# A fused retention and two-layer kernel: another order of products, sums and gates in the second layer, seven places for its weights, and fewer positions for preparing it

## The chip, the cores and the metric

One core of a Trainium2 chip runs the whole program. The metric is the device time of one execution in microseconds (us). TensorE is called PE below, VectorE DVE, ScalarE ACT, GpSimd POOL; SP is the engine whose queue issues nearly all transfers.

## What is computed

The reference, cut to what matters:

```python
# q, k, v: 4 batches, 8 heads, 576 tokens, 64 per head; x: 2304 tokens x 512
scores = q @ k.T / sqrt(64)
x = (scores * decay) @ v           # decay: causal, gamma(head) ** distance
h = x @ w_in;   x = relu(h) ** 2 @ w_out                  # 512 -> 2048 -> 512
h = x @ w_in2;  out = h * clip(h + 3, 0, 6) / 6 @ w_out2   # 512 -> 2048 -> 512
```

## The kernel before

**Precision.** A product keeps about float32 precision by splitting each operand into a high part (ACT copies it, rounded) and a low part (DVE or POOL subtracts, lines 200 and 201), and by adding three passes: high by high, high by low, low by high (`PASSES`). A "split" below is one such pair of instructions.

**Layer one** walks 64 positions i: four blocks of tokens (`FIRST`) by 16 chunks of 128 hidden channels. At position i, PE computes the hidden product `hps` of i (line 448) and then the output product `yps` of i - 2 (line 506). ACT makes relu, square and high part of i, DVE the low part `g` (line 477), then the split of the input weights `win` of i + 2. In the last three positions of a block the operands of the next block (`xring`, `xown`) are split too.

**Preparation.** Beside layer one, at the positions in `READY`, the weights of layer two are decoded from 64-bit numbers (`dec`: four DVE instructions, lines 179 to 194, and two on ACT), summed (`sums` on POOL, `out_sums` on DVE, lines 577 to 580), split into one of three places `ready`, and stored to DRAM (`kept`, `rights`). A pair of chunks takes four decodings, two groups of sums and eight splits. Each step has a cost in a planner's units (26 a decoding, 9 an output split, 176 a pair); the eight pairs' costs divided by the number of positions are the pace at which steps are handed out, in a fixed order.

**Layer two** uses a product scheme with seven products P1 to P7 in place of eight, in both of its matrix products, over three blocks j of 768 tokens. `hidden(j)` makes, for each of eight pairs p, seven products (line 723), combines them into `plain` and `mixed`, and closes them with the gate: `bend` (ACT, line 732) into a tile `v` of the pool `wo`, `close` (DVE, line 736). `sum_up(p)` (four DVE instructions, lines 674 and 677) then makes the summed operands. `plain` holds the operands of P1 and P2, which need no sums; P5 reads what the sums leave in `mixed`, and P6, P7 and P3 read `sums`. `visible(j)` runs the second seven products (line 870) in the order of `ORDER`, each in six entries s of 12 matmuls (left operand `gop`, split two entries ahead by `split_operand`) and four weight tiles of 512 KB (`load_right`, line 803), each used for one and a half entries. The pool `wo` has four places, which these weights share with `v`. Into the entries of `visible`, the lists `between` and `side` put other work: the last pair's gates and sums, and the operands and left weights (`load_left`, `win`, line 670) of the next block.

All instructions stand on their engines in the order in which the code writes them; an engine whose next instruction waits lets nothing behind it pass.

Of the kernel before, what the change touches and what calls it, by code (L numbers as in the profile page):

```python
# [9 lines left out]
F32 = mybir.dt.float32  # L10
# [12 lines left out]
HALF = 384  # L23
# [20 lines left out]

WARM = 18

READY = list(range(17, 59))

TOKENS = (("w4", "w5"), ("w6", "w7"), ("x4", "x5"), ("x6", "t7"), ("t0", "t1"), None, None)

# [27 lines left out]
def retention_moe_moe2(ctx, tc, qk, qk_last, kv, w_in, w_out, w_in2, w_out2, consts, out):  # L78
# [625 lines left out]


    def hidden(j, before):

        plain, mixed, sums = (later[x].tile([128, n, NPAIR, HALF], F32, tag=x, name=x) for x, n in
                              (("plain", 2), ("mixed", 2), ("sums", 3)))
        later["of", j] = {"P1": plain[:, 0], "P2": plain[:, 1], "P4": mixed[:, 0], "P5": mixed[:, 1],  # L710
                          "P6": sums[:, 0], "P7": sums[:, 1], "P3": sums[:, 2]}
        small = lambda k, p: dead(j, k)[:, HALF * (p % 2):HALF * (p % 2) + HALF]
        ta, tb, tc_, bent = {}, {}, {}, {}

        def product(p, name, to, first, last):
            k, half = LEFT[name]
            w = lefts[j, p, k] if k == 1 else lefts[j, p, k][:, half]
            x = operands[j, name]
            m = 0
            for f in range(2):  # L720
                o = slice(f * 128, f * 128 + 128)
                for wp, xp in PASSES:
                    nc.tensor.matmul(  # L723
                        out=to, lhsT=w[:, wp, o], rhs=x[:, xp, f],
                        start=first and m == 0, stop=last and m == 5, skip_group_check=True,
                    )
                    m += 1

        def bend(p, k):
            src = (plain, mixed)[k]  # L730
            v = bent[p, k] = wop.tile([128, 2, HALF], F32, tag="wo", name="v")
            nc.scalar.activation(out=v, in_=src[:, :, p], func=ACTF.Relu, bias=half_one, scale=1.0 / 6.0)  # L732

        def close(p, k):
            to = (plain, mixed)[k][:, :, p]
            nc.vector.scalar_tensor_tensor(
                out=to, in0=bent.pop((p, k)), scalar=1.0, in1=to, op0=ALU.min, op1=ALU.mult
            )

        def sum_up(p):  # L740
            less(sums[:, 1, p], plain[:, 0, p], mixed[:, 1, p])
            add(mixed[:, 1, p], mixed[:, 1, p], mixed[:, 0, p])
            less(sums[:, 0, p], mixed[:, 1, p], plain[:, 0, p])
            less(sums[:, 2, p], plain[:, 1, p], sums[:, 0, p])

        def fourth(p):
            product(p, "P4", ta[p], False, True)
            load_left(NPAIR * j + p + 2, 1) if p + 2 < NPAIR else None
            nc.scalar.activation(out=plain[:, 1, p], in_=ta[p], func=ACTF.Copy)
            bend(p, 0)  # L750

        def ahead(p, e):
            if p + 2 < NPAIR:
                load_left(NPAIR * j + p + 2, e)

        for p in range(NPAIR):
            ta[p], tb[p], tc_[p] = (bank(b + p % 2, [128, HALF], "hps") for b in (4, 2, 6))
            p1, p5, u2 = small(0, p), small(1, p), small(2, p)
            if p:
                bend(p - 1, 1)  # L760
            product(p, "P1", ta[p], True, False)
            nc.scalar.activation(out=p1, in_=ta[p], func=ACTF.Copy)  # L762
            if p > 1:
                sum_up(p - 2)
            product(p, "P5", tc_[p], True, False)
            nc.scalar.activation(out=p5, in_=tc_[p], func=ACTF.Copy)
            if p:
                close(p - 1, 1)
                fourth(p - 1)
            else:  # L770
                while unfinished:
                    unfinished.pop(0)()
            product(p, "P6", ta[p], False, False)
            nc.scalar.activation(out=u2, in_=ta[p], func=ACTF.Copy)
            if p:
                close(p - 1, 0)
            product(p, "P2", tb[p], True, True)
            ahead(p, 0)
            add(plain[:, 0, p], tb[p], p1)
            product(p, "P3", tc_[p], False, True)  # L780
            ahead(p, 3)
            add(mixed[:, 1, p], tc_[p], u2)
            product(p, "P7", ta[p], False, False)
            ahead(p, 2)
            add(mixed[:, 0, p], ta[p], p5)
            if p == NPAIR - 1:
                before()
        p = NPAIR - 1
        return [
            lambda: (bend(p, 1), sum_up(p - 1), close(p, 1)),  # L790
            lambda: (fourth(p), close(p, 0), sum_up(p)),
        ]

    ORDER = ["P1", "P5", "P6", "P2", "P7", "P3", "P4"]
    NQ = NPAIR // 2
    ENTRIES = NPAIR * HALF // 512
    FINAL = len(SECOND) - 1
    left_g, right_w = {}, {}

    def load_right(j, s):  # L800
        if s < len(ORDER) * NQ:
            w = wop.tile([128, 2, DM], F32R, tag="wo", name="wo")
            nc.sync.dma_start(out=w.bitcast(F32), in_=rights[s % NQ][:, ROW[ORDER[s // NQ]]])
            right_w[j, s] = w

    def split_operand(j, s):

        n, i = divmod(s, ENTRIES)
        if n >= len(ORDER):
            return  # L810
        if n < 4:
            t = place(f"w{i % 3}", [128, 2, 512], F32R, "gop")
        else:
            if (n, i) == (4, 0):
                later["entries"] = later["plain"].tile([128, ENTRIES, 2, 512], F32R, tag="plain", name="gop")
            t = later["entries"][:, i]
        left_g[j, s] = t
        src = later["of", j][ORDER[n]].rearrange("p a n -> p (a n)")[:, 512 * i:512 * i + 512]
        split_to(t[:, 0], t[:, 1], src, nc.vector)

    def visible(j, side, between):
# [38 lines left out]
        def multiply(n, u):  # L860
# [8 lines left out]
            for e, (gp, wp) in enumerate(PASSES):  # L869
# [3 lines left out]
                    stop=p == NPAIR - 1 and e == 2, skip_group_check=True,  # L873
                )

        due = {}
        for n, name in enumerate(ORDER):
            final = j == FINAL and n == len(ORDER) - 1
            for i in range(ENTRIES):
                s = n * ENTRIES + i  # L880
                if s + 2 < len(ORDER) * ENTRIES and s:
                    split_operand(j, s + 2)
                for f in due.pop(s, ()):
                    f()
                if final:
                    if i == 2:
                        for k in range(3, ENTRIES):
                            split_operand(j, n * ENTRIES + k) if (j, n * ENTRIES + k) not in left_g else None
                    continue
                for u in range(4 * i, 4 * i + 4):  # L890
                    multiply(n, u)
                    if u % 6 == 5:
                        load_right(j, n * NQ + u // 6 + 4)
                if s == 0:
                    split_operand(j, 2)
                if s < 2:
                    between[s]()
                for f in side.get(s, ()):
                    f()
            if not final:  # L900
                s = (n + 1) * ENTRIES
                due.setdefault(s, []).append(AFTER[name])
                if name in STORED:
                    due.setdefault(s + 3, []).extend(
                        lambda name=name, m=m: store(name, m, nc.sync) for m in range(3)
                    )
        if j == FINAL:
            n, name = len(ORDER) - 1, ORDER[-1]
            for m in range(3):
                for p in range(NPAIR):  # L910
                    multiply(n, 3 * p + m)
                one, two = spaces["a"]
                to = held(3)[:, m]
                if m == 1:
                    nc.vector.tensor_copy(to, one[:, 1])
                else:
                    nc.scalar.activation(out=to, in_=one[:, 0] if m == 0 else two, func=ACTF.Copy)
                store(name, m, (nc.sync, nc.scalar)[m % 2])
# [17 lines left out]
    with tc.manual_schedule():  # L936
# [229 lines left out]

        for j in range(len(SECOND)):

            def before():
                for s in range(2):  # L1170
                    split_operand(j, s)
                for s in range(3):
                    load_right(j, s)

            between = hidden(j, before)
            load_right(j, 3)
            side = {}
            if j < FINAL:
                for i, f in enumerate(operand_items(j + 1)):
                    side.setdefault(4 + 3 * i, []).append(f)  # L1180
                k = NPAIR * (j + 1)
                for i, e in enumerate((0, 3, 2, 1)):
                    side.setdefault(8 + 2 * i, []).append(lambda e=e: load_left(k + 1, e))
                    side.setdefault(26 + 2 * i, []).append(lambda e=e: load_left(k, e))
            visible(j, side, between)
        while unfinished:
            unfinished.pop(0)()
# [35 lines left out]
```

## Time and profile before

| | us |
|---|---|
| median of three runs | 868.62 (866.73 to 869.12) |
| the profiled execution | 868.59 |
| its span, first to last instruction | 866.8 |
| PE busy in the span | 829.6 (96%) |
| DVE, ACT, POOL busy | 611.9, 495.2, 145.1 |

The profile lists, for each engine, when it was busy, and for each gap which instruction or transfer released it. "Granted clock" is the share of PE's full clock that it was given in a stretch: 1.00 is 2.4 GHz, 0.50 is 1.2 GHz. A busy PE at half clock counts as busy.

### The profile page before, as it was taken

How to read it: one execution, taken by the hardware profiler on the slowest of the kernel's cores; microseconds unless marked ns; L12 is line 12 of the kernel's file. 1: busy time of each engine (PE TensorE's matmuls, PEld its weight loads, DVE VectorE, ACT ScalarE, POOL GpSimd, SP SyncE). 2: the span in 40 equal slices, each digit the busy share in tenths (PEclk: the TensorE clock that was granted, in tenths of full speed). 3: DMA queues.
4: the chain of work that ended last, by engine and by line, in shares of the span. 5: the costliest groups of instructions: out<-in, count | busy, mean ns of one | idle time of the engine just before them, and what ended most of it. 6: DMA issues, size and time to landing. Idle time of an engine off the chain costs nothing.

```text
span 866.8 us, 14891 instructions
## 1 busy us (share of the span) xinstructions
PE 829.6 (96%) x5580; PEld 750.3 (87%) x5580; DVE 611.9 (71%) x942; ACT 495.2 (57%) x895; POOL 145.1 (17%) x122
## 2 busy tenths in 40 slices
PE   8989999999999899989999998999998999998997
PEld 7878888888888688868887998999997999997996
DVE  5878777784798788799765677673678673678462
ACT  1238676776678668777855445463445462554451
POOL 2353232321343043134300000000000000000000
PEclk9999999999999899999999999899999999999998
DMA  9993566656778887988693774786875786774784
GB/s 361 346 304 113 174 195 174 192 193 205 279 255 287 285 279 252 331 257 292 246 343 138 236 256 147 240 282 255 265 252 157 261 265 241 264 255 147 212 266 130
DMA packets 80608, 208.74 MB, mean 241 GB/s; under 512 B 7958, under 2 KB 29078, under 8 KB 80536
## 3 DMA queue, kind: packets, MB, share of 16 engines
q1 hardware_dynamic: 80244, 207.52, 70.7%
q8 instruction: 44, 0.72, 0.3%
q14 instruction: 28, 0.23, 0.1%
q10 hardware_dynamic: 292, 0.27, 0.1%
HBM read 165.29 MB, written 42.47 MB: 240 GB/s over the span
## 4 chain that ended last, share of the span: by engine, by line
PE 66%; DMA 13%; DVE 10%; ACT 5%; issue 4%; POOL 2%; SPq 1%; DVEq 0%; ACTq 0%; POOLq 0%
PE hps L723 20%; PE yps L870 17%; PE hps L448 13%; PE yps L506 12%; DMA kvt<-in_kv_dram 4%; DMA wo<-rights 4%; PE ytail L506 2%; DMA kept<-ready 2%; DVE win L201 2%; DVE g L477 2%; DVE a L188 1%; DMA rights<-ready 1%; DVE a L182 1%; DVE a L179 1%; DMA win<-kept 1%
## 5 line engine op out<-in xcount | busy, mean ns | idle before, releaser
L870 PE MATMUL yps<-wo,gop 128*128 128x256 f32 x1512 | 196.5, 292 | 19.4 <-DVE gop L201 11.9
L870 PEld LDWEIGHTS yps<-wo,gop 128*128 128x128 f32 x1512 | 191.3, 198 | 24.4 <-DVE gop L201 13.1
L506 PE MATMUL yps<-g,wo 128*128 128x512 f32 x768 | 196.0, 394 | 0.9 <-POOL wo L201 0.9
L506 PEld LDWEIGHTS yps<-g,wo 128*128 128x128 f32 x768 | 141.5, 190 | 29.7 <-POOL wo L201 4.2
L448 PE MATMUL hps<-xring,win 128*128 128x512 f32 (+1 forms) x720 | 155.7, 364 | 5.0 <-DVE win L201 2.6
L448 PEld LDWEIGHTS hps<-xring,win 128*128 128x128 f32 x720 | 123.4, 190 | 27.9 <-DVE win L201 4.0
L723 PE MATMUL hps<-xlast,win 128*128 128x384 f32 x576 | 108.4, 334 | 0.7 <-DVE xlast L644 0.5
L723 PEld LDWEIGHTS hps<-xlast,win 128*128 128x128 f32 x576 | 100.4, 188 | 1.3 <-DVE xlast L644 0.8
L723 PE MATMUL hps<-xop,win 128*128 128x384 f32 x432 | 82.7, 334 | 0.4 <-ACT xall L762 0.4
L723 PEld LDWEIGHTS hps<-xop,win 128*128 128x128 f32 x432 | 75.5, 188 | 0.8 <-ACT xall L762 0.7
L477 DVE TENSOR_TENSOR g<-r,g 128x512 fp32r<-128x512 f32 x64 | 52.4, 819 | 31.6 <-ACT g L474 31.6
L732 ACT ACTIVATE v<-mixed,half_one 128x768 f32<-128x768 f32 x24 | 22.5, 939 | 74.3 <-DVE mixed L674 61.8
L470 ACT ACTIVATE r<-hps 128x512 f32<-128x512 f32 x80 | 43.5, 544 | 34.7 <-PE hps L448 31.9
L448 PE MATMUL hps<-xown,win 128*128 128x512 f32 x240 | 59.9, 390 | 1.5 <-DVE xown L201 1.5
L200 ACT ACTIVATE win<-w 128x512 fp32r<-128x512 f32 x64 | 39.7, 620 | 26.4 <-DVE w L194 26.4
L448 PEld LDWEIGHTS hps<-xown,win 128*128 128x128 f32 x240 | 44.8, 188 | 11.1 <-DVE xown L201 2.0
L179 DVE TENSOR_SCALAR a<-a 128x512 f32<-128x512 f32 x64 | 37.3, 584 | 22.5 <-ACT a L175 22.5
L188 DVE SCALAR_TENSOR_TENSOR a<-stage,a 128x512 int32<-128x512 int32 x64 | 50.4, 787 | 1.8
L473 ACT ACTIVATE r<-r 128x512 f32<-128x512 f32 x80 | 47.2, 590 | 2.5
L200 ACT ACTIVATE gop<-sums 128x512 fp32r<-128x512 f32 x54 | 32.7, 627 | 25.8 <-PE yps L870 23.2
L182 DVE TENSOR_SCALAR a<-a 128x512 int32<-128x512 int32 x64 | 45.4, 709 | 2.2
L200 ACT ACTIVATE gop<-mixed 128x512 fp32r<-128x512 f32 x37 | 23.3, 629 | 39.4 <-PE yps L870 37.3
(114 smaller groups left out, 1108.3 us busy)
## 6 DMA issues: line engine op xcount, KB each, us to landing
wo<-rights SPq DMA_DIRECT2D x84, 512.0 KB
win<-kept SPq DMA_DIRECT2D x72, 512.0 KB
wo<-kept SPq DMA_DIRECT2D x48, 512.0 KB
stage<-in_w_out_dram SPq DMA_DIRECT2D x32, 512.0 KB
kept<-ready SPq DMA_DIRECT2D x24, 512.0 KB
rights<-ready SPq DMA_DIRECT2D x24, 512.0 KB
kept<-wo SPq DMA_DIRECT2D x16, 512.0 KB
stage<-in_w_in_dram SPq DMA_DIRECT2D x16, 512.0 KB
```

Source lines behind the costliest of these rows:

```text
L179: nc.vector.tensor_scalar(out=a, in0=a, scalar1=LEAST, scalar2=MOST, op0=ALU.max, op1=ALU.min)
L182: nc.vector.tensor_scalar(out=a.bitcast(I32), in0=a.bitcast(I32), scalar1=3, scalar2=0x3FFFFFFF, op0=ALU.logical_shift_left, op1=ALU.bitwi ...
L188: nc.vector.scalar_tensor_tensor(out=a.bitcast(I32), in0=high, scalar=-0x40000000, in1=a.bitcast(I32), op0=ALU.bitwise_and, op1=ALU.bitwis ...
L200: lambda: nc.scalar.activation(out=hi, in_=src, func=ACTF.Copy),
L448: nc.tensor.matmul(out=h, lhsT=w[:, wp, kk * 128:kk * 128 + 128], rhs=xs[pos, kk][xp][:, o:o + n], start=m == 0, stop=m == 3 * KD - 1,)
L470: relu.append(lambda r=r, h=hs[k]: nc.scalar.activation(out=r, in_=h, func=ACTF.Relu))
L473: nc.scalar.activation(out=r, in_=r, func=ACTF.Square)
L477: low.append(lambda r=r, hi=hi, lo=lo: nc.vector.tensor_tensor(out=lo, in0=r, in1=hi.bitcast(F32), op=ALU.subtract))
L506: nc.tensor.matmul(out=p, lhsT=w[:, wp, m * 128:m * 128 + 128], rhs=g[pos, c][k][:, gpart, :size], start=c == 0 and e == 0 and not (k and ...
L723: nc.tensor.matmul(out=to, lhsT=w[:, wp, o], rhs=x[:, xp, f], start=first and m == 0, stop=last and m == 5, skip_group_check=True,)
L732: nc.scalar.activation(out=v, in_=src[:, :, p], func=ACTF.Relu, bias=half_one, scale=1.0 / 6.0)
L870: nc.tensor.matmul(out=acc, lhsT=t[:, gp, rows], rhs=w[:, 256 * wp:256 * wp + 256], start=name in ("P1", "P5", "P2") and u in (0, 2) and e ...
```

## The change

`READY` leaves out the last three and the first position of every block: 34 positions remain of 42. In `hidden`, the splits of the first three entries move into the last pair's products, the weight loads 0 to 3 ahead of its P2, and `sum_up` of pair 5 out of it. The gate of the last pair writes to a dead part of `xall` in place of a `wo` tile. `ORDER` takes P2 directly after P1. The sums of pairs 5, 6 and 7 come after entries 3, 5 and 7. From the third product on, the split operands take three places of a tile `spare` and the weights its three other places and the four of `wo`. The work for the next block starts at entry 9 (operands, before: 4) and at 15 (second half of the left weights, before: 26). The last product of the last block is run in the common order up to unit 18 and finished row by row.

```diff
-READY = list(range(17, 59))
+READY = [i for i in range(17, 59) if i % 16 not in (13, 14, 15, 0)]
...
         def bend(p, k):
             src = (plain, mixed)[k]
-            v = bent[p, k] = wop.tile([128, 2, HALF], F32, tag="wo", name="v")
+            if p == NPAIR - 1:
+                v = dead(j, 3).rearrange("p (a n) -> p a n", a=2)
+            else:
+                v = wop.tile([128, 2, HALF], F32, tag="wo", name="v")
+            bent[p, k] = v
...
-            if p > 1:
+            if p == NPAIR - 1:
+                before(0)
+            elif p > 1:
                 sum_up(p - 2)
...
                 close(p - 1, 1)
+                if p == NPAIR - 1:
+                    before(1)
                 fourth(p - 1)
...
+            if p == NPAIR - 1:
+                for s in range(4):
+                    load_right(j, s)
             product(p, "P2", tb[p], True, True)
...
+            if p == NPAIR - 1:
+                before(2)
             product(p, "P7", ta[p], False, False)
...
-            if p == NPAIR - 1:
-                before()
         p = NPAIR - 1
-        return [
-            lambda: (bend(p, 1), sum_up(p - 1), close(p, 1)),
-            lambda: (fourth(p), close(p, 0), sum_up(p)),
-        ]
-    ORDER = ["P1", "P5", "P6", "P2", "P7", "P3", "P4"]
+        return {
+            0: [lambda: bend(p, 1), lambda: close(p, 1)], 1: [lambda: fourth(p), lambda: close(p, 0)],
+            3: [lambda: sum_up(p - 2)], 5: [lambda: sum_up(p - 1)], 7: [lambda: sum_up(p)],
+        }
+    ORDER = ["P1", "P2", "P6", "P5", "P7", "P3", "P4"]
...
+        if s < ALONE or (s - ALONE) % 7 < 4:
             w = wop.tile([128, 2, DM], F32R, tag="wo", name="wo")
+        else:
+            w = spare(j)[:, 3 + (s - ALONE) % 7 - 4].rearrange("p (a n) -> p a n", a=2)
...
-        if n < 4:
+        if n < LONE:
             t = place(f"w{i % 3}", [128, 2, 512], F32R, "gop")
         else:
...
+            t = spare(j)[:, i % 3].rearrange("p (a n) -> p a n", a=2)
...
+        def ask(done):
+            while True:
+                s = asked[0] + 1
+                if s > done + (4 if s < ALONE + 4 else 7):
+                    return
+                if s >= ALONE + 4 and done < ALONE - 1:
+                    return
+                asked[0] = s
+                load_right(j, s)
...
-                    if u % 6 == 5:
-                        load_right(j, n * NQ + u // 6 + 4)
-                if s == 0:
-                    split_operand(j, 2)
-                if s < 2:
-                    between[s]()
-                for f in side.get(s, ()):
+                    if u % 6 == 5:
+                        ask(n * NQ + u // 6)
+                for f in between.get(s, []) + side.get(s, []):
                     f()
...
             for m in range(3):
-                for p in range(NPAIR):
+                for p in (6, 7):
                     multiply(n, 3 * p + m)
...
-                    side.setdefault(4 + 3 * i, []).append(f)
+                    side.setdefault(9 + 3 * i, []).append(f)
...
-                    side.setdefault(26 + 2 * i, []).append(lambda e=e: load_left(k, e))
+                    side.setdefault(15 + 2 * i, []).append(lambda e=e: load_left(k, e))
```

(`LONE` is 2 and `ALONE` is 8, the weight tiles of the first two products.)

**What stands where.** On DVE, behind the last pair's products of block j = 0. `sums<-plain,mixed` opens a `sum_up` of four rows, `v` is the bent gate, `gop` the low half of a split. Before:

```order
L677 TENSOR_TENSOR sums<-plain,mixed 128x384
L674 TENSOR_TENSOR mixed<-mixed 128x384
L677 TENSOR_TENSOR sums<-mixed,plain 128x384
L677 TENSOR_TENSOR sums<-plain,sums 128x384
L736 SCALAR_TENSOR_TENSOR mixed<-v,mixed 128x2x384
L201 TENSOR_TENSOR gop<-plain,gop 128x512
L736 SCALAR_TENSOR_TENSOR plain<-v,plain 128x2x384
L677 TENSOR_TENSOR sums<-plain,mixed 128x384
L674 TENSOR_TENSOR mixed<-mixed 128x384
L677 TENSOR_TENSOR sums<-mixed,plain 128x384
L677 TENSOR_TENSOR sums<-plain,sums 128x384
L201 TENSOR_TENSOR gop<-plain,gop 128x512 x2
```

Now, from the last pair's second gate on:

```order
L740 SCALAR_TENSOR_TENSOR mixed<-xall,mixed 128x2x384
L201 TENSOR_TENSOR gop<-plain,gop 128x512
L740 SCALAR_TENSOR_TENSOR plain<-xall,plain 128x2x384
L201 TENSOR_TENSOR gop<-plain,gop 128x512 x2
L677 TENSOR_TENSOR sums<-plain,mixed 128x384
L674 TENSOR_TENSOR mixed<-mixed 128x384
L677 TENSOR_TENSOR sums<-mixed,plain 128x384
L677 TENSOR_TENSOR sums<-plain,sums 128x384
L201 TENSOR_TENSOR gop<-plain,gop 128x512 x2
L677 TENSOR_TENSOR sums<-plain,mixed 128x384
```

Two splits stand between the last gate and the first sums now, where the sums of the last pair stood ahead of them.

On DVE again, in layer one at the end of a block: `xring` is the next block's operand, `a` and `wd` are a decoding. Before:

```order
L201 TENSOR_TENSOR xring<-xall,xring 128x512
L477 TENSOR_TENSOR g<-r,g 128x512
L201 TENSOR_TENSOR win<-w_491,win 128x512
L179 TENSOR_SCALAR a<-a 128x512
L182 TENSOR_SCALAR a<-a 128x512
L188 SCALAR_TENSOR_TENSOR a<-stage,a 128x512
L194 ISA wd<-a,r 128x1024
L201 TENSOR_TENSOR xring<-xall,xring 128x512 x2
```

Now:

```order
L201 TENSOR_TENSOR xring<-xall,xring 128x512
L477 TENSOR_TENSOR g<-r,g 128x512
L201 TENSOR_TENSOR win<-w_491,win 128x512
L201 TENSOR_TENSOR xring<-xall,xring 128x512 x2
```

The decoding between the operands' splits has gone to positions inside the blocks.

## Rows read from the trace of the kernel before

**Rows 1.** What PE waited for, whole span (total us, times, longest), largest five.
```profile
PE yps L870 <- DVE gop L201: 11.9, 6, 2.9
PE yps L870 <- DMA wo<-rights: 6.2, 11, 1.3
...
PE hps L448 <- DVE win L201: 2.6, 3, 1.4
PE hps L448 <- DVE xring L201: 2.4, 1, 2.4
PE hps L448 <- DVE xown L201: 1.5, 1, 1.5
```

**Rows 2.** Chain that ended last, layer two (start us, us, what, count).
```profile
475.77 55.41 PE hps L723 x318
...
565.98 8.87 PE yps L870 x72
...
602.93 57.22 PE hps L723 x330
...
732.17 57.22 PE hps L723 x330
...
856.27 7.41 PE yps L870 x48
```

**Rows 3.** Order of time, start of `visible(0)` (start us, us, engine, line, operation; idle before).
```profile
532.41 2.89 PE L870 MATMUL yps<-wo,gop 128*128 128x256 f32 x22 [1.01 <-DVE gop L201]
...
534.62 0.94 ACT L732 ACTIVATE v<-mixed,half_one 128x768 f32<-128x768 f32 x1 [4.18 <-PE yps L870]
...
535.14 1.21 PE L723 MATMUL hps<-xlast,win 128*128 128x384 f32 x6
...
536.38 0.49 ACT L749 ACTIVATE plain<-hps 128x384 f32<-128x384 f32 x1 [0.30 <-PE hps L723]
...
538.83 0.96 DVE L736 SCALAR_TENSOR_TENSOR plain<-v,plain 128x768 f32<-128x768 f32 x1 [1.55 <-ACT v L732]
...
539.83 0.63 ACT L200 ACTIVATE gop<-plain 128x512 fp32r<-128x512 f32 x1 [0.51 <-DVE plain L736]
539.83 0.56 DVE L677 TENSOR_TENSOR sums<-plain,mixed 128x384 f32<-128x384 f32 x1
...
542.08 1.28 DVE L201 TENSOR_TENSOR gop<-plain,gop 128x512 fp32r<-128x512 f32 x2
...
542.82 5.49 PE L870 MATMUL yps<-wo,gop 128*128 128x256 f32 x24 [2.95 <-DVE gop L201]
```

**Rows 4.** Stretches of 2 us: length, busy us by engine, granted clock, DMA share, GB/s.
```profile
286.00:288.00 2.00, 1.13 (x3) 0.94 (x4) 2.00 (x5) 0.42 (x1) 0.00 (x0) 0.50 1.07 392
288.00:290.00 2.00, 2.00 (x6) 1.54 (x5) 1.97 (x6) 0.60 (x1) 0.00 (x0) 0.50 0.98 352
...
292.00:294.00 2.00, 2.00 (x8) 1.60 (x8) 1.86 (x4) 0.89 (x2) 0.00 (x0) 0.79 0.57 223
544.00:546.00 2.00, 2.00 (x12) 2.00 (x11) 0.84 (x1) 0.63 (x1) 0.00 (x0) 0.50 0.45 82
```

**Rows 5.** PE in order of time, where layer one waits.
```profile
286.87 2.50 PE L448 MATMUL hps<-xring,win 128*128 128x512 f32 x5 [2.38 <-DVE xring L201]
```

**Rows 6.** Stretches of a position (busy PE, PEld, DVE, ACT, POOL), and 41 positions' sum.
```profile
309.94:315.38 5.44, 5.44 (x25) 4.50 (x24) 5.27 (x6) 4.34 (x9) 4.43 (x3) 1.00 0.53 157
...
320.82:326.26 5.44, 5.44 (x25) 4.50 (x24) 2.81 (x5) 1.50 (x3) 0.00 (x0) 1.00 1.02 411
...
sum 233.39, PE 226.93 PEld 185.92 DVE 194.75 ACT 168.10 POOL 77.93; mean PE 5.53 PEld 4.53 DVE 4.75 ACT 4.10 POOL 1.90
```

**Rows 7.** PE in order of time, inside the last block of layer one.
```profile
434.16 1.19 PE L448 MATMUL hps<-xring,win 128*128 128x512 f32 x4 [0.32 <-DVE win L201]
```

**Rows 8.** What ACT waited for from 200 to 434 us (total us, times, longest).
```profile
ACT ready L200 <- DMA kept<-ready: 28.6, 14, 3.8
```

**Rows 9.** A stretch of `visible(0)` with transfers at their densest.
```profile
585.68:590.12 4.44, 3.64 (x31) 3.47 (x30) 4.20 (x7) 2.13 (x4) 0.00 (x0) 1.00 1.03 415
```

More of the change, by code (lines that the diff above doesn't have):

```diff
@@ L798, in retention_moe_moe2, with spare @@
     left_g, right_w = {}, {}
+    LONE = 2
+    ALONE = LONE * NQ
     def load_right(j, s):
-        if s < len(ORDER) * NQ:
+        if s >= len(ORDER) * NQ:
+            return
+        if s < ALONE or (s - ALONE) % 7 < 4:
             w = wop.tile([128, 2, DM], F32R, tag="wo", name="wo")
-            nc.sync.dma_start(out=w.bitcast(F32), in_=rights[s % NQ][:, ROW[ORDER[s // NQ]]])
-            right_w[j, s] = w
+        else:
+            w = spare(j)[:, 3 + (s - ALONE) % 7 - 4].rearrange("p (a n) -> p a n", a=2)
+        nc.sync.dma_start(out=w.bitcast(F32), in_=rights[s % NQ][:, ROW[ORDER[s // NQ]]])
+        right_w[j, s] = w
+    def spare(j):
+        if ("spare", j) not in later:
+            later["spare", j] = later["plain"].tile([128, ENTRIES, 1024], F32R, tag="plain", name="gop")
+        return later["spare", j]
     def split_operand(j, s):
@@ L810, in split_operand @@
             return
-        if n < 4:
+        if n < LONE:
             t = place(f"w{i % 3}", [128, 2, 512], F32R, "gop")
         else:
-            if (n, i) == (4, 0):
-                later["entries"] = later["plain"].tile([128, ENTRIES, 2, 512], F32R, tag="plain", name="gop")
-            t = later["entries"][:, i]
+            t = spare(j)[:, i % 3].rearrange("p (a n) -> p a n", a=2)
         left_g[j, s] = t
@@ L874, in multiply @@
                 )
+        asked = [3]
+        def ask(done):
[4 more added lines that the diff above has]
+                if s >= ALONE + 4 and done < ALONE - 1:
+                    return
+                asked[0] = s
+                load_right(j, s)
         due = {}
@@ L880, in visible @@
                 s = n * ENTRIES + i
-                if s + 2 < len(ORDER) * ENTRIES and s:
+                if s:
                     split_operand(j, s + 2)
@@ L884, in visible @@
                     f()
[L885 to L889, printed above, removed]
                 for u in range(4 * i, 4 * i + 4):
+                    if final and u >= 18:
+                        break
                     multiply(n, u)
                     if u % 6 == 5:
-                        load_right(j, n * NQ + u // 6 + 4)
-                if s == 0:
-                    split_operand(j, 2)
-                if s < 2:
-                    between[s]()
-                for f in side.get(s, ()):
+                        ask(n * NQ + u // 6)
+                for f in between.get(s, []) + side.get(s, []):
                     f()
@@ L1167, in retention_moe_moe2, with before @@
         for j in range(len(SECOND)):
[L1169 to L1173, printed above, removed]
+            def before(k):
+                split_operand(j, k)
             between = hidden(j, before)
-            load_right(j, 3)
             side = {}
```

## The prediction

> **What bounds the kernel now.** I read the waits of PE first, since PE is busy for 829.6 of 866.8 us and the rest is mostly its waiting. Two waits stand out, on split operands of layer two (11.9 us) and on its weights (6.2); three belong to layer one (2.6, 2.4 and 1.5) [rows 1]. Second the chain that ended last, which gives the borders of the stages. Third the order of time at one border, which tells why PE waits there. Fourth the granted clock around the long waits: PE runs at half clock, 1.2 GHz, behind them [rows 4], so a wait costs more than its length.
>
> Layer two, stage by stage. `hidden` ran without a gap in all three blocks: 57.22 us where nothing waited [rows 2]. `visible` did not. From the end of `hidden(0)` at 475.77 + 55.41 = 531.18 to the next `hidden` at 602.93 are 71.75 us; the second stage takes 732.17 - 660.15 = 72.02; the third runs from 789.39 to its last matmul at 856.27 + 7.41 = 863.68, so 74.29 [rows 2]. At full clock 72 matmuls take 8.87 us [rows 2], 0.123 each; the 504 of a stage take 62.1, and the last pair's P4 product some 1.0 more, so 63.1 is the floor of a stage. The three stages are above it by 8.65, 8.9 and 11.2, 28.75 us in all. That sum holds the waits and the half clock behind them.
>
> Why they wait is in [rows 3]. The last pair's first gate is bent at 534.62, 4.18 us late by PE, since its tile takes a place of `wo` that an early weight holds. Behind it on ACT stands the copy of P4 (536.38), then the second gate; DVE closes that at 538.83, makes four sum instructions from 539.83 to 542.08, and only then the low halves of the next splits. PE waits 2.95 us for those, and runs at 0.50 afterwards [rows 3, 4].
>
> **The change in `visible`.** Call T the end of the last pair's products. The splits of entries 0 to 2 now stand inside those products; DVE there loses one `sum_up` (2.25 us, 539.83 to 542.08 [rows 3]) and gains three low halves at 0.64 (1.28 for two [rows 3]), so that stretch should stay without a gap, and the first wait (1.01 [rows 3]) goes. The gate's tile is dead memory, so nothing on ACT waits for a weight. I follow DVE from there with durations of [rows 3]. PE does entries 0 and 1 by T + 2.96 (12 matmuls are 1.48), then P4; the copy follows 1.24 after P4's start (535.14 to 536.38), at T + 4.2, takes 0.49; the gate is bent in 0.94 and closed from T + 5.7 to 6.65 (0.96). From here DVE has no rest: low halves 4 and 5 (to 8.0, the second held by ACT's half, 0.63), sums of pair 5 (to 10.25), halves 6 and 7 (11.5), sums of pair 6 (13.75), halves 8 and 9 (15.0), sums of pair 7 (17.25), half 10 at 17.9. PE needs half 4 at about 7.2, half 6 at 10.3, half 8 at 13.85 and half 10 at 17.35, each pushed back by the wait before it (an entry can make two of its 12 matmuls with the high half alone). So four short waits remain where there were two long ones: about 0.1, 0.6, 0.55 and 0.55, **1.8 us a stage**. None nears the 2.95 that stood ahead of the half clock. After half 10 DVE is ahead again: per entry it owes 0.64 of 1.48 and every third entry 0.96 for the next block.
>
> **The weights.** With four places a tile is asked for three tiles (6.7 us of PE) ahead; the chain shows transfers of about that length, and PE waited on them 6.2 us in all [rows 1]. With seven places it is asked for six tiles (13.3 us) ahead. The eight left weights of the next block now come in entries 8 to 22, over 20.7 us of PE, closer together than before: in this time are asked 12.3 weight tiles (9.3 at the common pace and the three of `spare` at once), eight left weights and three stores, 10.5 MB. At the 415 GB/s of the densest stretch [rows 9] these need 25.3 us, so transfers fall 4.6 us behind, inside the cover of 13.3. I put **0.2 us a stage** here, between nothing and the present 2.1 (a third of 6.2). The Trainium skill speaks against this: its page "DMA: Bandwidth & Descriptors" (Bandwidth) says that some 358 GB/s bind between HBM and SBUF. By that figure the lag would be 8.6 us, still inside the cover; the trace's 415 disagrees with it and decides.
>
> The last block also had its last product taken row by row, with all four weights wanted within the first row; now 18 of its 24 units run in the common order, and each row's end is three matmuls for each of two pairs. What follows the last matmul (copy and store, 866.8 - 863.7 = 3.1) stays.
>
> So the stages go from 28.75 above their floor to 3 x 2.0 = 6.0: **-22.75 us**. Bounds: 1.0 a stage (half of my DVE chain hides) gives -25.75; 3.9 a stage (all present transfer waits stay) gives -17.
>
> **The change in layer one.** At the borders PE waited 2.6 + 2.4 + 1.5 = 6.5 us [rows 1], all but the 0.32 of [rows 7] at the two borders, where DVE had decodings between the next block's splits; at the first, 2.38 us for `xring` [rows 5] was followed by half clock: three stretches of 2 us at 0.50 and one at 0.79 (first, second and last are in [rows 4]), less the 0.87 of waiting in the first, some 3.0 us lost. With those positions free of preparation DVE owes there two halves and at most two splits, 2.6 of 5.44 us. So **-9.2 us**, if nothing takes its place.
>
> What may take its place: the same work in 34 positions. A pair had 5.25 positions (28.6 us), now 4.25 (23.1). DVE was busy 194.75 us in 41 positions [rows 6]; two halves a position (1.28) and a dozen border instructions (some 7.7) leave 134.5 for preparation, 16.8 a pair. In 4.25 positions DVE has 23.1 - 5.4 = 17.7 for it: it fits, 96% full. ACT stood 28.6 us waiting for a place `ready` to be stored [rows 8], 3.6 a pair, and DVE waits behind it at the end of each pair, as in the light position 320.82 (busy 2.81 at a DMA share of 1.02 [rows 6]). If all of it stays, DVE falls 2.7 behind per pair. A split of `win` is due some 4.9 us after DVE can have it: two positions (10.9) less half a position, three ACT steps and two halves. A block of 12 positions holds 2.8 pairs, so 7.6 late, of which PE feels 2.7; the shorter last block feels 1.5. That makes 7 us. Bursts add to it: two decodings in one position, followed by the sums, is the pattern of the 0.32 us wait [rows 7]; by the planner's costs it stood at two positions (33 and 54) and now stands at six. At 0.3 to 1.0 each, 2 to 6 more. So the cost lies between nothing (DVE fits) and 13. I take **+4.5**, nearer the lower end, since a late DVE finds its transfers landed, so lateness and the wait for a place overlap.
>
> **Sum.** The profiled execution took 868.59, the median is 868.62, so one stands for the other: 868.6 - 22.75 - 9.2 + 4.5 = 841.2 us, rounded to **841**.
>
> **Rivals.**
>
> *The preparation does not fit.* The 13 us above, and a wait in each of the three blocks long enough for half clock, 3.0 each: 22 in place of 4.5, so 858; half of that 850. For it: PE had as little as 0.32 us too little in a single burst. Against: DVE's busy sum fits. Chance 0.17.
>
> *The short waits still bring half clock.* One wait of 2.38 us did so at 287 us [rows 4, 5]; four that add up to 1.8 within 11 us might: about 3.0 a stage, 841 + 9 = 850. For it speaks the Trainium skill, "TensorE: Matmul & The Clock Gate" (A second HAM failure mode), by which PE idling briefly but often between groups made the clock swing. Against it: behind the 1.01 us wait 22 matmuls took 2.89 us, the full rate [rows 3]. Chance 0.10.
>
> *The weights still wait*, because left weights, a burst of three and stores share one queue in order: 2.1 - 0.2 = 1.9 in the two stages that load ahead, 845. Chance 0.05.
>
> *Slower: a pair needs its 28.6 us whatever its positions.* Decoding, sums, three places and stores follow one another; if their chain is serial, each of eight pairs is 5.5 us late, 44 in all, of which three blocks hide 4.9 each: 29.3 of waiting, and with half clock behind every pair (8 x 3.0) 53 against 32 gained, 890. It decides from 32 us on, which is some 27 us a pair. Against it: DVE had 28.6 - 16.8 - 6.7 = 5.1 us a pair to spare and was busy 2.81 of 5.44 in a light position [rows 6], so the chain has slack. Chance 0.03.
>
> That the order is not what the words say is excluded by the rows of the order: sums stand behind splits, gates write to `xall`.
>
> **Chances.** Forecast 0.65 (834 to 846), the rivals 0.17, 0.10, 0.05 and 0.03. A tenth may lie above 853 and a twelfth below 833 (floor of everything: 868.6 - 25.75 - 9.2 = 833.6), so the range is 833 to 853. Faster by over 0.3% (2.6 us, about what a measurement here can tell from no change) 0.95, within 0.02, slower 0.03.
>
> **What would show it.** Right: `visible` takes about 65 us in each block; the waits on `gop` are some four per stage, all under 0.8, between T + 7 and T + 18; no stretch of layer two below clock 1.00; waits on weights under 1 us in all; no wait on `xring` or `xown`. The waits on `win` or `wo` inside blocks, near the pattern of two decodings, tell what I paid for packing: 4.5 us is right, over 10 the first rival. Wrong at once: a `hidden` above 57.5, or a granted clock of 0.50 inside a block.

## The result, and the profile after

The changed kernel takes **856.6 us** (median, 855.6 to 857.2) against 867.7 for the kernel before: a ratio of 0.987, interval 0.985 to 0.989. The forecast was 841, its range 833 to 853. The kernel became faster, by less than half of what was forecast. Layer two did what the sum said; layer one took more than half of it back.

The chain that ended last gives the stages, as in [rows 2] (start us, us, what, count); the profiled execution took 856.5 us, its span 854.7:

```profile
489.16 55.39 PE hps L723 x318
544.56 2.87 PE yps L891 x24
...
608.31 57.20 PE hps L723 x330
```

The first and the last but one give `visible(0)`: 608.31 - 544.56 = 63.75 us, where 71.75 stood in [rows 2]. But `hidden(0)` begins at 489.16 and not at 475.77, 13.4 us later. From there to the end of the span are 365.5 us, before 391.0: layer two gained **25.5 us**. In front of it, from the first hidden product of block two to `hidden(0)`, these two rows (before, then after; order of time on PE) tell the other half:

```profile
191.60 2.91 PE L448 MATMUL hps<-xown,win 128*128 128x512 f32 x12
```

```profile
190.00 2.91 PE L448 MATMUL hps<-xown,win 128*128 128x512 f32 x12
```

Blocks two to four took 475.77 - 191.60 = 284.2 us before and 489.16 - 190.00 = 299.2 after: **15.0 us longer**. (Block one, which the change does not touch, ended 1.6 earlier; over all the kernels below it ends between 188.8 and 191.6.) 25.5 - 15.0 + 1.6 = 12.1, the difference of the two spans.

What PE waited for (total us, times, longest), as in [rows 1]:

```profile
PE hps L448 <- ACT win L200: 7.8, 7, 2.6
PE hps L448 <- DVE win L201: 7.6, 9, 1.6
PE yps L891 <- DVE gop L201: 3.6, 9, 0.6
```

The waits on `gop` fell from 11.9 to 3.6, those on weights `wo` and on the next block's operands are gone. New are 15.4 us of waits on the input weights `win` inside layer one's blocks, where before only 0.32 us of such waiting stood away from the borders. They are of two kinds: on ACT's half and on DVE's half of the split. And this is what ACT waited for in layer one, as in [rows 8], here from 200 to 465 us:

```profile
ACT ready L200 <- DMA kept<-ready: 48.8, 23, 5.7
...
ACT ready L200 <- DMA rights<-ready: 6.5, 4, 2.7
```

That is 55.3 us in which ACT stood in front of a split whose place `ready` was still being stored. Over the same stretch of the kernel before, the first row has the 28.6 of [rows 8] and the second is

```profile
ACT ready L200 <- DMA rights<-ready: 7.5, 5, 3.4
```

so 36.1 us in all. (An expectation below says 33: it counted only up to 434 us.)

### The profile page after: what moved, and what is told of

Read it like the earlier page. It is cut to its first block, busy times and chain, and to the rows that moved or that the text cites. A ratio compares the mean times of both kernels' runs of the same rounds, so it can differ in the third digit from the quotient of the medians.

```text
span 854.7 us, 14951 instructions
## 1 busy us (share of the span) xinstructions
PE 823.9 (96%) x5580; PEld 740.2 (87%) x5580; DVE 609.9 (71%) x941; ACT 495.1 (58%) x894; POOL 144.4 (17%) x122
## 4 chain that ended last, share of the span: by engine, by line
PE 64%; DVE 11%; DMA 10%; ACT 7%; issue 4%; POOL 3%; SPq 1%; ACTq 0%; DVEq 0%; POOLq 0%
PE hps L723 20%; PE yps L891 16%; PE hps L448 12%; PE yps L506 11%; DMA kept<-ready 4%; PE ytail L506 2%; DVE sums L677 2%; DMA stage<-in_w_in_dram 2%; DMA kvt<-in_kv_dram 1%; DVE gop L201 1%; DVE a L188 1%; DVE win L201 1%; ACT r L473 1%; POOL ready L201 1%; DVE g L477 1%
## 5 line engine op out<-in xcount | busy, mean ns | idle before, releaser
L448 PE MATMUL hps<-xring,win 128*128 128x512 f32 (+1 forms) x720 | 159.9, 369 | 9.6 <-ACT win L200 5.2
L891 PE MATMUL yps<-wo,gop 128*128 128x256 f32 x1080 | 134.8, 284 | 3.8 <-DVE gop L201 3.6
L891 PEld LDWEIGHTS yps<-wo,gop 128*128 128x128 f32 x1080 | 131.4, 192 | 6.5 <-DVE gop L201 6.1
L448 PE MATMUL hps<-xown,win 128*128 128x512 f32 x240 | 62.0, 395 | 6.3 <-DVE win L201 3.5
L736 ACT ACTIVATE v<-mixed,half_one 128x768 f32<-128x768 f32 x21 | 19.7, 938 | 61.9 <-DVE mixed L674 61.9
L891 PE MATMUL yps<-gop 128*128 128x256 f32 x432 | 53.6, 283 | 0.5 <-ACT xall L944 0.5
L891 PEld LDWEIGHTS yps<-gop 128*128 128x128 f32 x432 | 52.5, 192 | 0.7 <-ACT xall L944 0.7
L201 DVE TENSOR_TENSOR gop<-sums,gop 128x512 fp32r<-128x512 f32 x54 | 36.4, 689 | 22.3 <-ACT gop L200 22.3
```

Of the source, the lines that this page charges most:

```text
L201: lambda: lo_engine.tensor_tensor(out=lo, in0=src, in1=hi.bitcast(F32), op=ALU.subtract),
L448: nc.tensor.matmul(out=h, lhsT=w[:, wp, kk * 128:kk * 128 + 128], rhs=xs[pos, kk][xp][:, o:o + n], start=m == 0, stop=m == 3 * KD - 1,)
L891: nc.tensor.matmul(out=acc, lhsT=t[:, gp, rows], rhs=w[:, 256 * wp:256 * wp + 256], start=name in ("P1", "P5", "P2") and u in (0, 2) and e ...
```

## The experiments

Ten kernels, each timed beside the kernel before (medians of 865.9 to 868.1); the ratio is to that neighbour. "Blocks" is the length from block two's first hidden product to `hidden(0)` in the profiled execution, read as above.

| kernel | us | ratio to before, interval | blocks |
|---|---|---|---|
| before | 867.7 | | 284.2 |
| after | 856.6 | 0.987 (0.985 to 0.989) | 299.2 |
| after, 42 positions | 841.3 | 0.970 (0.967 to 0.973) | 282.6 |
| before, 34 positions | 877.7 | 1.012 (1.009 to 1.016) | 300.5 |
| after, four places | 846.2 | 0.976 (0.972 to 0.979) | 288.5 |
| after, one decoding a position | 865.0 | 0.997 (0.994 to 0.999) | 306.1 |
| after, four places, one decoding | 849.9 | 0.979 (0.976 to 0.983) | 294.3 |
| after, four places, 42 positions | 833.4 | 0.960 (0.957 to 0.964) | 275.9 |
| after, four places, one decoding, 38 positions | 835.3 | 0.962 (0.959 to 0.965) | 278.8 |
| after, 42 positions, weights in four places | 845.5 | 0.974 (0.972 to 0.977) | 283.7 |
| before, four places | 858.4 | 0.991 (0.987 to 0.995) | 276.2 |
| after, four places, no clamp | 838.2 | 0.968 (0.963 to 0.973) | 279.2 |

**Which half of the change lost it.** One kernel undoes the positions alone:

```diff
-READY = [i for i in range(17, 59) if i % 16 not in (13, 14, 15, 0)]
+READY = list(range(17, 59))
```

> The changed kernel with the 42 preparation positions of before: only the change in layer two is left. If the miss lies in the packing of the preparation, layer one runs as in the kernel before and the time is what layer two gives alone: 868 less some 25, 842 to 845 us, faster than the changed kernel by 12 to 15, with waits on the next block's operands at the borders (about 6 us) back. The rival, that layer two or the start of the program took the missing 15 us, expects no more than the 9 us worse that the borders were worth: 860 to 866.

841.3 us. The waits in the blocks are gone; what is left in layer one, 5.7 us in three rows, stands nearly all at the borders, as before:

```profile
PE yps L891 <- DVE gop L201: 3.6, 9, 0.6
PE hps L448 <- DVE xring L201: 2.6, 1, 2.6
...
PE hps L448 <- DVE win L201: 1.6, 2, 1.4
PE hps L448 <- DVE xown L201: 1.5, 1, 1.5
```

So layer two alone is worth 26 us, and the 34 positions cost 15.3. The reverse, the kernel before with the 34 positions:

```diff
-READY = list(range(17, 59))
+READY = [i for i in range(17, 59) if i % 16 not in (13, 14, 15, 0)]
```

> The kernel before with the 34 positions alone. If packing is the cause, this is slower than before by what layer one lost in the changed kernel: 868 + 15 = 881 to 884 us, with some 15 us of waits on the input weights inside the blocks. If the packing alone is harmless and only together with the new layer two costs time, about 860 to 869.

877.7 us, slower than before; its blocks took 300.5 us, 16.3 longer, about as much as in the changed kernel. The packing costs what it costs without any help from layer two. Its total is 3 us better than expected, since its unchanged layer two took 387.1 us in place of 391.0. The waits on `gop` are the same (11.9 us in six); PE was busy for less, at a higher mean clock (before, then this kernel; length, busy us by engine, granted clock, DMA share, GB/s):

```profile
475.77:866.80 391.03, 368.52 (x2508) 363.27 (x2508) 244.98 (x386) 182.83 (x308) 0.00 (x0) 0.97 0.69 229
```

```profile
491.24:878.30 387.06, 364.81 (x2508) 359.79 (x2508) 245.00 (x386) 182.80 (x308) 0.00 (x0) 0.99 0.68 231
```

**The place.** One more place for the prepared splits, in a part of memory that is free in these blocks:

```diff
-            t = in_turn("bounce", "t3", 3, [128, 1024], "ready")
+            t = bounce_place()
...
+    def bounce_place():
+        turn["bounce"] += 1
+        return place(("t3", "t4", "t5", "x4")[turn["bounce"] % 4], [128, 1024], F32R, "ready")
```

> The changed kernel with four places in place of three for the split, prepared weights on their way to memory. If what packing costs is ACT standing in order behind a split whose place is still being stored (55 us of such waits in layer one after, 33 before), a fourth place takes most of the 7.8 us of PE's waits on ACT's halves away, and the half clock behind the two longest: 856 goes to 845 to 850. If DVE's bursts are the cause, the waits on DVE's halves (7.6 us) and nearly the whole time stay: 853 to 857.

(Both lines that ask for a place are changed so.) 846.2 us: 10.4 gained. No wait on ACT's half is left, and ACT's own waits for a place halve; what PE still waits for in the blocks is DVE's half (line numbers are four higher here):

```profile
PE hps L452 <- DVE win L205: 10.3, 9, 2.2
PE yps L895 <- DVE gop L205: 3.6, 9, 0.6
```

```profile
ACT ready L204 <- DMA kept<-ready: 25.7, 12, 5.1
```

**The bursts.** The hand-out stops at a second decoding in a position:

```diff
+                decoded = 0
-                while ready and owed > ready[0][0] / 2:
+                while ready and owed > ready[0][0] / 2 and decoded + (ready[0][0] == 26) < 2:
...
+                    decoded += cost == 26
```

> The changed kernel, with the same 34 positions and the same pace, but never more than one decoding in a position: the rest of a position's due goes to the next. If the six positions with two decodings cause PE's waits on DVE's halves (7.6 us in nine waits), these fall to some 2 us and the time to 848 to 852. If the sum of DVE's work in a block is the cause, whatever the order within it, the waits stay as long in total: 855 to 858.

865.0 us, above both ranges: 8.4 slower than without the edit. The waits went as the first alternative said, the time did not. Waits on DVE's half fell from 7.6 to 1.3, but those on ACT's half rose from 7.8 to 19.9:

```profile
PE hps L448 <- ACT win L200: 19.9, 7, 4.8
...
PE hps L448 <- DVE win L201: 1.3, 2, 0.7
```

A step put off does not vanish: by the planner's costs, position 37 for instance now gets the fourth decoding of a pair together with its output sums and all four output splits, which had two positions before. With four places as well (this edit and the one before it together), the two causes were to be shown separate:

> The changed kernel with both: four places for the split, prepared weights, and at most one decoding in a position. Alone the fourth place took the 7.8 us of waits on ACT away and left 10.3 on DVE; alone the single decoding took the waits on DVE from 7.6 to 1.3 and raised those on ACT to 19.9. If the two are separate causes, with lateness of one handed to the other only through the places, both go: waits on the input weights under 3 us in layer one, and 834 to 839 us, the fastest so far. If it is the sum of work in 34 positions that does not fit, the waits turn up again on some engine, 8 to 12 us of them: 844 to 850.

They are not: 849.9 us, slower than four places alone. ACT now stands in front of splits whose decoding DVE has not finished:

```profile
PE hps L452 <- ACT win L204: 7.2, 5, 4.1
PE hps L452 <- DVE win L205: 4.2, 5, 1.7
```

```profile
ACT ready L204 <- DVE wd L198: 21.9, 6, 4.4
ACT ready L204 <- DMA kept<-ready: 17.3, 12, 3.4
```

So my theory of two independent causes fell. In 34 positions the lateness moves from engine to engine, as its rival said (8 to 12 us of waits; 11.4 measured).

**How much too much.** Four places, and one DVE instruction of each decoding left out in layer two's weights:

```diff
-            nc.vector.tensor_scalar(
-                out=a, in0=a, scalar1=LEAST, scalar2=MOST, op0=ALU.max, op1=ALU.min
-            )
+            if l == 0:
+                nc.vector.tensor_scalar(
+                    out=a, in0=a, scalar1=LEAST, scalar2=MOST, op0=ALU.max, op1=ALU.min
+                )
```

> The changed kernel (34 positions, two decodings allowed) with four places and without the first instruction of DVE's four in layer two's decodings, the clamp (0.42 us, longer beside POOL): part of the computation is left out, 32 instructions and some 13 us of DVE. If what is left of the waits (10.3 us on DVE's halves of the input weights) is DVE having more work in 34 positions than time, they fall by most of what was taken out per burst: to 3 to 6 us, and 839 to 842. If it is the order (a split standing behind others' waits, not DVE's time), they stay: 844 to 847.

838.2 us, 8.0 below the same kernel with the clamp. DVE is busy for 206.15 us in the blocks in place of 220.72, so 14.6 less, and the waits on DVE's half go from 10.3 us to 1.6 (0.8 stand on ACT): 8.7 us of them are gone. Behind the places, it is DVE's time that does not fit. (A decoding without the clamp is also ready sooner; this run does not tell the sum of DVE's work from the length of its chain.)

**More positions, with the fourth place.** The edit of the place and the one of the 42 positions together:

> The changed kernel with the 42 positions of before and four places: what the fourth place is worth where the preparation is not packed. If the waits at the borders come from DVE's decodings between the next block's splits, which a place does not move, 839 to 842, hardly below 841.3. If ACT's standing behind a place also made the borders late, the 5.7 us of waits there and their half clock go: 833 to 837.

**833.4 us**, the fastest of all, 4.0% below the kernel before and 2.7% below the changed one. One border wait is left:

```profile
PE hps L452 <- DVE xring L205: 1.4, 1, 1.4
```

Two positions less at each border, the place and one decoding a position:

```diff
-READY = [i for i in range(17, 59) if i % 16 not in (13, 14, 15, 0)]
+READY = [i for i in range(17, 59) if i % 16 not in (14, 15)]
```

> Four places, one decoding at most, and 38 positions: only the last two of each block without preparation. If the borders need two free positions and the blocks some more room, this is the best of all: 832 to 837, with neither border waits nor waits in the blocks above 2 us. If three free positions are needed at a border, the waits on the next block's operands come back with 2 to 3 us: 838 to 842.

835.3 us: no wait on the next block's operands, but 2.4 us on `win`, of which 2.0 stand in the last position of block two, one of those left free. It is within 2 us of the former, neither much better than 42 positions nor worse. And the kernel before with the place alone:

> The kernel before with the fourth place alone. If what its borders lost (6.5 us of waits and some 3 us of half clock) came in the main from ACT standing behind a place, as the run with 42 positions and four places suggests (one wait of 1.4 us left), this gains as much as there: some 8 us, 859 to 861, with one wait of about 1.4 us at the first border. If there it was the new layer two that made the difference, 865 to 869.

858.4 us, 7.6 below its neighbour. Of its border waits only the one on `xring` stays (2.3 us), and those on `win` and `xown` are gone; its blocks took 276.2 us, 8.0 less, and ACT's waits for a place are 16.1 us in place of 36.1. Thus most of what [rows 1] shows as border waits came of the three places, and a fourth one cures it without moving anything.

**The seven places of the weights.** Layer two as changed, 42 positions, all weights in the four places of `wo`, asked for four ahead:

```diff
-        if s < ALONE or (s - ALONE) % 7 < 4:
+        if True:
...
-                if s > done + (4 if s < ALONE + 4 else 7):
+                if s > done + 4:
```

> The changed layer two (with 42 positions) without the seven places: all weights of the second products take the four places of the pool and are asked for four ahead, as before the change. If the seven places are what ended the waits on weights (6.2 us in the kernel before, none after), these come back with 3 to 6 us: 845 to 848. If the order and the straight last product did it, and four places do where nothing is taken row by row, 841 to 843.

845.5 us, 4.2 more than with seven (841.3). The waits are back, 3.8 us in the two stages that also load the next block's left weights; those of the first are:

```profile
565.74 6.70 PE L891 MATMUL yps<-wo,gop 128*128 128x256 f32 x54 [2.24 <-DMA wo<-rights]
573.06 24.02 PE L891 MATMUL yps<-wo,gop 128*128 128x256 f32 x198 [0.61 <-DMA wo<-rights]
```

## Why the prediction was wrong, point by point

**`visible`: right.** The forecast was 65 us a stage. The first two took 63.75 and 63.76 at full clock (length, busy us by engine, granted clock, DMA share, GB/s), the third 64.8 to its last matmul:

```profile
544.56:608.31 63.75, 62.52 (x511) 61.71 (x511) 46.75 (x72) 33.76 (x55) 0.00 (x0) 1.00 0.78 283
665.52:729.28 63.76, 62.52 (x511) 61.70 (x511) 46.76 (x72) 33.75 (x55) 0.00 (x0) 1.00 0.78 283
```

The chain that I followed by hand can be laid beside the rows of order of time from T = 544.56:

```profile
548.51 0.49 ACT L753 ACTIVATE plain<-hps 128x384 f32<-128x384 f32 x1 [1.76 <-PE hps L723]
549.03 0.94 ACT L736 ACTIVATE xall<-plain,half_one 128x768 f32<-128x768 f32 x1
...
550.00 0.96 DVE L740 SCALAR_TENSOR_TENSOR plain<-xall,plain 128x768 f32<-128x768 f32 x1 [2.19 <-ACT xall L736]
...
555.32 3.13 PE L891 MATMUL yps<-wo,gop 128*128 128x256 f32 x24 [0.56 <-DVE gop L201]
...
558.76 3.14 PE L891 MATMUL yps<-wo,gop 128*128 128x256 f32 x24 [0.32 <-DVE gop L201]
...
562.22 3.98 PE L891 MATMUL yps<-wo,gop 128*128 128x256 f32 x31 [0.31 <-DVE gop L201]
```

The copy of P4 stood at T + 3.95 (forecast 4.2), the closing gate at T + 5.4 (5.7). The first short wait did not come, the others ended at T + 10.8, 14.2 and 17.7 with 0.56, 0.32 and 0.31 in place of 0.6, 0.55 and 0.55: 1.2 us a stage for 1.8. PE came to them when the sum said (T + 10.2, 13.9 and 17.35); DVE's halves were some 0.2 us earlier. The floor was set too high as well: PE was busy for 62.5 us a stage, where I had put 63.1. So layer two gained 25.5 us for 22.75, inside the bounds. The rival of half clock behind short waits did not happen: no stretch of layer two is below 1.00 from its start to its last matmuls.

**The weights: right.** No wait on them is left, where I had put 0.2; the kernel with the weights in four places says that the seven are worth 4.2 us.

**The borders: right in the result, wrong in the reason.** No wait on `xring` or `xown` is left after. But I had laid these to DVE's decodings between the next block's splits. With all these decodings where they were and a fourth place, 1.4 to 2.3 of the 6.5 us remain. The wait on `xring` at the first border may be of that kind (a decoding still stands in front of its split); the others went with the place.

**Packing: the step that failed.** The sum put 4.5 us, between nothing and 13. Measured: blocks two to four are 15.0 us longer, where by the sum the free borders make them 9.2 shorter, so in the sum's terms packing cost some **24 us**. Both signs that the prediction had named came: over 10 us of waits on `win` in the blocks (15.4), and a clock of 0.50 inside a block. Two of the term's working assumptions were wrong.

First, "a late DVE finds its transfers landed, so lateness and the wait for a place overlap", my ground for the value near the lower end. ACT's waits for a place rose from 36.1 to 55.3 us. It is ACT that stands there, in order, and its next instructions are relu and square of the current position. The row and its wake, order of time:

```profile
247.43 1.07 SPq L431 DMA_DIRECT2D kept<-ready  x2
...
255.03 0.42 ACT L200 ACTIVATE ready<-wd 128x256 fp32r<-128x256 f32 x1 [5.67 <-DMA kept<-ready]
...
256.29 0.58 ACT L470 ACTIVATE r<-hps 128x512 f32<-128x512 f32 x1
...
258.77 3.38 PE L448 MATMUL hps<-xown,win 128*128 128x512 f32 x12 [1.10 <-ACT win L200]
```

ACT waits 5.67 us for a place. Three places in turn means the place of the split three before, and that one's store was issued at 247.43 and is done 7.6 us later, beside other transfers (DMA share 0.91 from 246 to 252 us, 1.03 from 252 to 258). Relu of a product that ended at 248.8 runs only at 256.29, the half of `win` behind it is late, and PE waits 1.10. The same 64 splits had to pass three places in 34 positions: with 42 positions the same waits of ACT are 39.0 us. The fourth place took 10.4 us of the loss away. (The sum also had this wait too small: its 28.6 us, 3.6 a pair, are the stores to `kept` alone; with the 7.5 for `rights` it is 4.5 a pair, and the 7 us of lateness become some 14 by the same sum.)

Second, "it fits, 96% full" (16.8 of 17.7 is 95%). A busy sum over 34 positions says nothing of the one engine's place in a chain that runs from DVE over POOL and ACT to the stores and back to DVE, and so little slack did not suffice. With four places the loss that stays is DVE's (10.3 us of waits), and taking 14.6 us of its time out removes 8.7 of them. The bursts were seen, but as a small addition; limiting decodings to one a position did not smooth them away, as the two kernels with it show.

The loss in PE's own terms, blocks two to four of before and then of after (length, busy us by engine, clock, DMA share, GB/s):

```profile
191.60:475.70 284.10, 276.68 (x1214) 227.09 (x1212) 222.13 (x328) 196.30 (x355) 80.57 (x66) 0.99 0.75 264
```

```profile
190.00:489.10 299.10, 282.36 (x1214) 225.84 (x1212) 221.18 (x328) 196.74 (x355) 80.36 (x66) 0.99 0.72 251
```

The same 1,214 matmuls: 9.3 us more of idle time (16.7 for 7.4) and 5.7 us more of busy time. There is half clock in it, behind the two longest waits:

```profile
336.00:338.00 2.00, 2.00 (x7) 1.52 (x6) 1.83 (x4) 1.97 (x4) 0.00 (x0) 0.50 0.26 78
...
364.00:366.00 2.00, 2.00 (x6) 1.52 (x6) 1.79 (x5) 1.94 (x4) 0.00 (x0) 0.50 0.52 198
```

But with the stretches beside these (0.95, 0.70, 0.77 and 0.87) it comes to some 3 us, as much as the kernel before lost at its first border [rows 4]. So the 5.7 us are not the clock's. A wait costs more than its length at full clock too: the 12 matmuls of 258.77, behind a wait, took 3.38 us at 1.00, those of 190.00 took 2.91.

So the outcome was the first rival, "the preparation does not fit", at nearly its full price: it gave 858 and a chance of 0.17. Its own upper price (22 us) had been worked out from rows; the mistake was to weigh it down by an overlap that no row showed. That 858 came so near is in part luck: its three spells of half clock, 9 us, were two and some 3 us, and layer two gained 2.75 us more than the sum had. The slower rival (890) was not reached, though the change of positions by itself is slower than the kernel before (877.7).

What stays open: how much of DVE's share is its slowing beside POOL. In the kernel with four places, six of the nine waits on DVE's half, 9.5 of the 10.3 us, come right behind a low half of `win` that took 1.2 to 1.8 us while POOL was working; elsewhere the same instruction takes 0.69:

```profile
250.18 0.69 DVE L205 TENSOR_TENSOR win<-w,win 128x512 fp32r<-128x512 f32 x1
...
366.88 2.87 POOL L205 TENSOR_TENSOR ready<-wd,ready 128x512 fp32r<-128x512 f32 x2
...
367.40 1.75 DVE L205 TENSOR_TENSOR win<-w,win 128x512 fp32r<-128x512 f32 x1
...
369.21 0.97 PE L452 MATMUL hps<-xring,win 128*128 128x512 f32 x3 [2.24 <-DVE win L205]
```

No kernel here took POOL's part away, so this is a rival to "too much work" that is not tried.

## What to carry to other kernels

Work fitted in beside a bounding engine was limited here by the handovers of its chain, so cost such work by how long its instructions hold up what stands behind them on each in-order engine, not by the busy sum of one. Before moving such work away from a place where the bounding engine waits, ask whether that wait began earlier, at a buffer: here one more place of 4 KB a partition gave 8 to 10 us in three kernels and 15 with one decoding a position, while freeing eight positions lost 15 without that place and still 13 with it (846.2 against 833.4). A change of two independent parts should be priced, and tried, as two.

## What the runs showed of the hardware that had not been expected

The length of a wait does not tell whether PE falls to half clock. In the changed kernel a wait of 1.88 us was followed by 0.50 (336 to 338 us, shown above):

```profile
334.66 4.95 PE L448 MATMUL hps<-xring,win 128*128 128x512 f32 x12 [1.88 <-ACT win L200]
```

In the kernel with four places the wait of 2.24 us that ended at 369.21 left the clock at 1.00 in the same and the next stretch:

```profile
368.00:370.00 2.00, 0.79 (x3) 0.67 (x4) 2.00 (x2) 1.94 (x5) 2.00 (x3) 1.00 0.30 119
370.00:372.00 2.00, 2.00 (x10) 1.65 (x9) 1.93 (x3) 1.09 (x3) 1.18 (x1) 1.00 1.00 256
```

Nor does the same wait always cost the same. Behind the wait of 2.9 us on `gop` in `visible(0)`, the kernel before stood at 0.50 in three stretches of 2 us and at 0.79 in a fourth (542 to 550 us); the kernel before with 34 positions had this, and 1.00 again from 564 us:

```profile
558.00:560.00 2.00, 1.71 (x12) 1.71 (x13) 2.00 (x4) 0.18 (x1) 0.00 (x0) 0.90 0.04 12
560.00:562.00 2.00, 2.00 (x11) 2.00 (x11) 1.00 (x2) 0.45 (x1) 0.00 (x0) 0.50 0.85 262
562.00:564.00 2.00, 2.00 (x15) 2.00 (x15) 0.69 (x1) 1.39 (x3) 0.00 (x0) 0.75 0.27 53
```
